# A decode kernel whose last weight matrix arrives in five shrinking pieces, and whose end code is aligned to 256 instructions

## The chip, the cores and the metric

One core of a Trainium2 chip. The metric is device time in microseconds (us) of one execution. Times inside a trace are us from the start of the span, which runs from the first to the last instruction of the program. The measured time is about 2 us longer than the span (1273.29 against 1271.6 us for the profiled run of before).

## The reference, cut to what matters

Two rows of activations pass through grouped-query attention over a key and value cache of 32768 positions, and through a small GELU layer; a gate mixes the two.

```python
q = x @ wq                       # 2 x 1 x 448  ->  16 heads of 256
scores = einsum(q, k) * 256**-0.5    # 8 KV heads, 32768 keys, for each of 2 batch rows
a = einsum(softmax(scores), v).reshape(2, 1, 4096) @ wo     # wo: 4096 x 448
b = gelu(x @ w1 + b1) @ w2 + b2
out = g * a + (1 - g) * b            # g = sigmoid(sum(x * gate_w))
```

The two caches are 537 MB of the 547 MB that must be read.

## The kernel before

SyncE issues every large load on one queue, far ahead of its use: 32 K tiles and 32 V tiles of 8 MB through three slots of SBUF, then the last V tile in three pieces, W2, and WO in four pieces.

```python
    PIECES = (64, 32, 32)                # the last V tile
    WOP = (0, 16, 28, 31, 32)            # WO: bounds of its pieces, in column blocks
    ...
                elif kind == "WO":
                    src = A_wo.rearrange("(p c) n -> p (c n)", p=P)
                    for i in range(len(WOP) - 1):
                        c0, c1 = WOP[i] * Dm, WOP[i + 1] * Dm
                        dma(lambda e, src=src, c0=c0, c1=c1: e.dma_start(wo_v[:, c0:c1], src[:, c0:c1]), f"pW{i}", ("wo", i))
```

TensorE consumes a piece as soon as it is there, two matmuls for each of the 32 blocks:

```python
            def FIN(i):
                E.wait(f"pW{i}", ("wo", i))
                for c in range(WOP[i], WOP[i + 1]):
                    for q in range(2):
                        E.ins(lambda e, c=c, q=q: e.matmul(
                            ps_a[64 * q:64 * q + Bn, :], attnT[:, c:Bn * NC:NC],
                            wo_v[:, c * Dm + q * DQ:c * Dm + (q + 1) * DQ], start=False, ...
```

VectorE, ScalarE and TensorE run a loop over the tiles and then straight code for the end ("tail"). SyncE's program has no loop. VectorE's end, for example:

```python
            for i in range(LAG):
                K(i)
            E.loop((NTILES - LAG) // UNIT, steps, ("dve", ("PT", 0)))
            do_end(NG - 1)               # opens with two copies (selg, o_sb), then waits for the last V pieces
            E.wait("pe", ("OT", NG - 1))
            ...
            E.wait("pe", "FIN")
            E.ins(lambda e: e.tensor_copy(out_sb[:, 0:DQ], ps_a[0:Bn, :]), key="mixd", stream="mix")
```

Of the kernel before, what the change touches and what calls it, by code (L numbers as in the profile page):

```python
# [11 lines left out]
class _Stream:  # L12
    def __init__(self, name, inc):
        self.name = name
        self.inc = inc
        self.count = 0
        self.total = None
        self.events = {}
        self.sem = None
# [7 lines left out]
class _Eng:  # L27
    def __init__(self, sched, name):
        self.s = sched
        self.name = name  # L30
        self.eng = None
        self.log = None
        self.at = None

    def dyn(self, base, step):

        return base if self.at is None else self.at[0] * step + base
# [88 lines left out]
def bass_gated_mix__gqa_block_cached__dense_activation_gelu__decode_kernel(  # L126
# [53 lines left out]
    assert (NTILES - LAG) % UNIT == 0  # L180
    PIECES = (64, 32, 32)
    NC = HD // P
    WOP = (0, 16, 28, 31, 32)
    DQ = Dm // 2
    GELU_C = 0.7978845608028654
    GELU_A = 0.044715
# [7 lines left out]
    for i in range(len(PIECES)):  # L194
        sch.stream(f"pV{i}", 16)
    for i in range(len(WOP) - 1):
        sch.stream(f"pW{i}", 16)
# [3 lines left out]
    with contextlib.ExitStack() as es:  # L201
# [62 lines left out]
        def grp(g):  # L264
            return g // Hkv, g % Hkv
# [74 lines left out]
        def prog_pool(E):  # L340
            E.ins(lambda e: e.memset(ident_b[:], 0.0), key="ms0")
            E.ins(lambda e: e.memset(ident_f[:], 0.0), key="ms1")
            E.ins(lambda e: e.memset(ones_f[:], 1.0), key="ones")
            E.ins(lambda e: e.memset(xm[:], 0.0), key="xm0")
            E.wait("pool", "ms0")
            E.ins(lambda e: e.affine_select(out=ident_b[:], in_=ident_b[:], compare_op=ALU.not_equal, fill=1.0,
                                          base=0, pattern=[[-1, P]], channel_multiplier=1), key="idb")
            E.wait("pool", "ms1")
            E.ins(lambda e: e.affine_select(out=ident_f[:], in_=ident_f[:], compare_op=ALU.not_equal, fill=1.0,
                                          base=0, pattern=[[-1, P]], channel_multiplier=1), key="idf")  # L350
            E.ins(lambda e: e.memset(Abd[:], 0.0), key="A0")
            E.ins(lambda e: e.memset(tsel[:], 0.0), key="t0")
            E.wait("pool", "t0")
            for b in range(Bn):
                E.ins(lambda e, b=b: e.affine_select(
                    out=tsel[:, 136 * b:136 * b + 136], in_=tsel[:, 136 * b:136 * b + 136], compare_op=ALU.not_equal,
                    fill=1.0, base=256 - 128 * b, pattern=[[-1, 136]], channel_multiplier=-8), key=f"ts{b}")

        def prog_sp(E):
            def dma(fn, stream, key):  # L360
                E.ins(fn, key=key, stream=stream)

            for d in order:
                for pd in before_of[d]:
                    E.wait("pe", released(pd))
                kind, idx = d
                if kind == "WQ":
                    parts = [(wq_f, A_wq[0:KC * P, :].rearrange("(p k) n -> p (k n)", p=P), "d_wq0"),
                             (wq_r, A_wq[KC * P:Dm, :].rearrange("p (h n) -> (p h) n", h=2), "d_wq1")]
                    for i, (o, src, _) in enumerate(parts):  # L370
                        dma(lambda e, o=o, src=src: e.dma_start(o, src), "slot0", ("wq", i))
                elif kind == "W1":
                    parts = [(w1_f, B_w1[0:KC * P, :].rearrange("(p k) n -> p (k n)", p=P)),
                             (w1_r, B_w1[KC * P:Dm, :].rearrange("p (h n) -> (p h) n", h=2))]
                    for i, (o, src) in enumerate(parts):
                        dma(lambda e, o=o, src=src: e.dma_start(o, src), "d_w1", ("w1", i))  # L376
                elif kind == "W2":
                    dma(lambda e: e.dma_start(w2_f, B_w2.rearrange("(p f) n -> p (f n)", p=P)), "d_w2", "w2")
# [5 lines that stand above are left out]
                elif d == ("V", LASTV):  # L384
                    src, base, r0 = kv_src(A_v_cache, idx), slot_of[d] * SLOT, 0
                    for i, n in enumerate(PIECES):
                        c0, c1 = r0 * Dh, (r0 + n) * Dh
                        dma(lambda e, c0=c0, c1=c1: e.dma_start(ring[:, base + c0:base + c1], src[:, c0:c1]),
                            f"pV{i}", ("piece", i))
                        r0 += n  # L390
                else:
                    src = kv_src(A_k_cache if kind == "K" else A_v_cache, idx)
                    dma(lambda e, src=src, d=d: e.dma_start(cut(slot_of[d], 0, SLOT), src),
                        f"slot{slot_of[d]}", ("fill", d))
            E.wait_total("mix")
            dma(lambda e: e.dma_start(out[:, 0, :], out_sb), "d_out", "out")
            E.wait_total("d_out")

        def prog_pe(E):
# [147 lines left out]
# [4 lines that stand above are left out]
# [43 lines left out]
            E.wait("dve", "at")  # L594
            for i in range(len(WOP) - 1):
                FIN(i)

        def prog_act(E):
# [35 lines left out]
            def chain(g):  # L634
                E.wait("pe", ("M2", g))
                E.ins(lambda e: e.mul(negm[:, :], ps_m[:, C_BC:C_BC + 1], -SCALE), key=("NM", g))  # L636
                E.wait("act", ("NM", g))
                if g >= 1:
                    E.wait("dve", ("PT", g - 1))
                E.ins(lambda e: e.activation(pexp[:, :].rearrange("p (r i a) -> p i r a", r=CR, i=2),  # L640
                                             ps_s[:, :].rearrange("p (i r a) -> p i r a", i=2, r=CR), ACTF.Exp, bias=negm[:, 0:1], scale=SCALE,
                                             accum_out=lsum[:, 0:1]), key=("X", g))
# [9 lines left out]
            fill_A(1)  # L652
            E.loop(NG - 2, step, ("dve", ("PT", 0)))
            chain(NG - 1)
            E.wait("pe", "FIN")
            E.ins(lambda e: e.copy(out_sb[:, DQ:Dm], ps_a[64:64 + Bn, :]), key="mixa", stream="mix")

        def prog_dve(E):
# [82 lines left out]
            def do_end(g):  # L741
                b, kvh = grp(g)
                if g < NG - 1:
                    E.wait("pe", ("PV", g * NT + NT - 1))
                E.wait("pe", ("OT", g - 1))
                E.wait("dve", "sel")
                E.ins(lambda e: e.tensor_copy(selg[:, :], selw[:, bass.ds(E.dyn(2 * g, 2 * UNIT // NT), 32)]), key=("SG", g))
                E.ins(lambda e: e.tensor_copy(o_sb[:, Dh:Dh + 1], ls3[:, g % 3:g % 3 + 1]), key=("OL", g))
                for n in range(8):
                    w, i = n // 2, n % 2  # L750
                    if g == NG - 1 and i == 0 and w > 0:
                        if w > 1:
                            E.wait("pe", ("PV", LASTV) if w == 3 else ("PVp", w))
                    p = ps_o[:, 512 * w + 256 * i:512 * w + 256 * i + 256]
                    m = mask[:, 4 * i + w:4 * i + w + 1]
                    if n == 0:
                        E.wait("dve", "mask")
                        if g == NG - 1:
                            E.wait("pe", ("PVp", 1))
                        E.ins(lambda e, p=p, m=m: e.tensor_scalar(o_sb[:, 0:Dh], p, m, None, op0=ALU.mult), key=("OS0", g))  # L760
                    else:
                        E.wait("dve", ("OS" + str(n - 1), g))
                        E.ins(lambda e, p=p, m=m: e.scalar_tensor_tensor(  # L763
                            out=o_sb[:, 0:Dh], in0=p, scalar=m, in1=o_sb[:, 0:Dh], op0=ALU.mult, op1=ALU.add),
                            key=(("OS" if n == 7 else "OS" + str(n)), g))
# [15 lines left out]
            for i in range(LAG):  # L781
                K(i)
            E.loop((NTILES - LAG) // UNIT, steps, ("dve", ("PT", 0)))
            do_end(NG - 1)
            E.wait("pe", ("OT", NG - 1))
            E.ins(lambda e: e.reciprocal(rinv[:, :], ps_oa[:, Dh:Dh + 1]), key="ri")
# [55 lines left out]
```

## Time and profile before

| | before |
|---|---|
| time, median of the first 3 runs | 1273.29 us (1273.07 to 1273.34) |
| span of the profiled run | 1271.6 us |
| TensorE / VectorE busy | 55% / 54% |
| main DMA queue | 547.43 MB, 99.6% of 16 engines' span |

The page of the kernel before, its DMA part: for each queue the packets, the megabytes and the time of its packets as a share of 16 DMA engines' span.

```profile
q1 hardware_dynamic: 10804, 547.43, 99.6%
q8 instruction: 8, 0.13, 0.0%
...
q14 instruction: 3, 0.02, 0.0%
```

By this page the packets of queue 1 alone fill 99.6% of the 16 DMA engines' span, so nothing but the start and the end of the stream can be shortened. I read the packets of the two "instruction" queues as fetches of the program itself; with 0.13 and 0.02 MB of 547.59 they are nothing by bytes. Queue 8 I take for TensorE's.

The timeline of the kernel before, its end: start, duration, engine, line, operation, and in brackets the idle time before with what ended it.

```profile
1262.09 2.78 PE L459 MATMUL ps_f<-ring,hT_bf 128*2 128x224 bf16 x28
...
1264.76 2.14 PE L551 MATMUL ps_f<-ring,attnT 128*2 128x224 bf16 x32
...
1267.90 1.70 PE L551 MATMUL ps_f<-ring,attnT 128*2 128x224 bf16 x32 [1.00 <-DMA ring<-in_A_wo_dram]
1269.64 0.34 ACT L656 CAST pexp<-ps_f 2x224 bf16<-2x224 f32 x1 [45.75 <-PE ps_f L551]
1269.64 0.38 DVE L793 CAST pexp<-ps_f 2x224 bf16<-2x224 f32 x1 [7.21 <-PE ps_f L551]
1270.05 0.33 SPq L396 DMA_DIRECT2D out_dram<-pexp  x1
```

TensorE waits 1.00 us for WO's second piece and then has half of WO, 32 matmuls, still to do before the two casts.

### The profile page before, as it was taken

The page shows a single profiled execution, that of the slowest core. Times are in us where ns is not written, and L with a number is a line of the kernel's source. Part 1 is how long each engine was busy: PE and PEld are TensorE (multiplying, and loading weights), DVE is VectorE, ACT ScalarE, POOL GpSimd, SP SyncE. Part 2 cuts the span into 40 slices and gives each one's busy share as a digit, 9 for nine tenths or more (in the row PEclk, how much of TensorE's full clock was granted, in tenths as well). Part 3 has the DMA queues.
Part 4 walks back from the last instruction along what each step waited for, and adds up shares of the span by engine and source line. Part 5 has one row for each costly group of instructions (what it writes and reads, how often), then busy time and mean ns, then how long its engine had stood idle before and what let it go on. Part 6 is the DMA issues. An engine that isn't in the chain of part 4 may idle for free.

```text
span 1271.6 us, 8088 instructions
## 1 busy us (share of the span) xinstructions
PE 698.9 (55%) x4544; PEld 146.0 (11%) x2016; DVE 685.8 (54%) x528; ACT 43.7 (3%) x183; POOL 3.3 (0%) x14
## 2 busy tenths in 40 slices
PE   4566566644466443665544665455664437655465
PEld 3111011100011100111100111000110001111012
DVE  2875537655365563556735466453755636566341
ACT  1000000000000000000000000000000000000000
POOL 1000000000000000000000000000000000000000
PEclk9988788767887777887778887778876778877686
DMA  9999999999999999999999999999999999999998
GB/s 404 441 434 431 429 429 435 431 439 434 431 429 435 437 431 437 435 431 429 433 439 431 437 435 429 431 433 439 431 437 433 431 431 433 439 431 433 437 423 359
DMA packets 10971, 547.59 MB, mean 431 GB/s; under 512 B 1352, under 2 KB 1616, under 8 KB 1872
## 3 DMA queue, kind: packets, MB, share of 16 engines
q1 hardware_dynamic: 10804, 547.43, 99.6%
q8 instruction: 8, 0.13, 0.0%
q10 hardware_dynamic: 156, 0.01, 0.0%
q14 instruction: 3, 0.02, 0.0%
HBM read 547.43 MB, written 0.00 MB: 431 GB/s over the span
## 4 chain that ended last, share of the span: by engine, by line
DMA 63%; DVE 21%; PE 13%; issue 3%; SPq 0%; another core or an unknown queue 0%
DMA ring<-in_A_k_cache_dram 60%; DVE ring L722 19%; PE ps_o L335 4%; PE ps_s L490 3%; PE ps_s L335 3%; DMA ring<-in_A_wo_dram 3%; DVE mx L726 1%; PE ps_o L539 1%; PE ps_m L499 0%; PE ps_m L504 0%; DVE gmax L728 0%; DVE gmx L732 0%; PE ps_f L551 0%; SPq L376 0%
## 5 line engine op out<-in xcount | busy, mean ns | idle before, releaser
L722 DVE STREAM_TRANSPOSE ring<-ring 128x2048 uint32<-128x2048 uint32 x256 | 565.2, 2275 | 390.2 <-DMA ring<-in_A_k_cache_dram 389.9
L490 PE MATMUL ps_s<-ring,Abd 128*128 128x512 bf16 x1024 | 427.0, 417 | 428.7 <-DVE ring L722 428.3
L335 PE MATMUL ps_s<-ring,Abd 128*128 128x512 bf16 x1024 | 423.3, 413 | 0.0
L490 PEld LDWEIGHTS ps_s<-ring,Abd 128*128 128x128 bf16 x1024 | 106.1, 104 | 852.0 <-DVE ring L722 480.1
L335 PE MATMUL ps_o<-ring,PT 128*24 128x512 bf16 x1504 | 112.9, 408 | 0.0
L539 PE MATMUL ps_o<-ring,PT 128*24 128x512 bf16 x544 | 58.1, 427 | 12.6 <-DMA ring<-in_A_v_cache_dram 12.6
L509 PE MATMUL ps_f<-o_sb,selg 128*32 128x257 f32 x32 | 17.0, 634 | 83.5 <-DVE o_sb L763 83.5
L763 DVE SCALAR_TENSOR_TENSOR o_sb<-ps_o,mask,o_sb 128x256 f32<-128x256 f32 x112 | 54.1, 483 | 8.9 <-PE ps_o L539 5.0
L726 DVE TENSOR_REDUCE mx<-ps_s 128x1 f32<-128x1024 f32 x16 | 19.6, 1224 | 59.9 <-PE ps_s L335 59.9
L636 ACT ACTIVATE negm<-ps_m 128x1 f32<-128x1 f32 x16 | 2.7, 171 | 1156.4 <-PE ps_m L504 1156.4
L739 DVE STREAM_TRANSPOSE PT<-pexp 128x1024 bf16<-128x1024 bf16 x16 | 19.9, 1245 | 36.8 <-PE ps_o L335 36.8
L539 PEld LDWEIGHTS ps_o<-ring,PT 128*24 128x24 bf16 x544 | 14.7, 100 | 104.1 <-issue 86.9
L736 DVE COPY ls<-lsum 128x1 f32<-128x1 f32 x16 | 2.5, 154 | 31.8 <-ACT pexp L640 31.8
L630 ACT COPY Abd<-qrep 32x16 bf16 (+1 forms) x128 | 19.4, 199 | 0.6
L640 ACT ACTIVATE pexp<-ps_s,negm 128x1024 bf16<-128x1024 f32 x16 | 17.8, 1113 | 1.7
L499 PE MATMUL ps_m<-ident_f,mx 128*1 128x128 f32 x32 | 6.1, 271 | 21.1 <-DVE mx L726 21.1
L760 DVE TENSOR_SCALAR o_sb<-ps_o,mask 128x256 f32<-128x256 f32 x16 | 7.6, 475 | 17.7 <-PE ps_o L335 17.7
L509 PEld LDWEIGHTS ps_f<-o_sb,selg 128*32 128x32 f32 x32 | 2.9, 139 | 101.6 <-DVE o_sb L763 99.5
L504 PE MATMUL ps_m<-ones_f,gmx 1*128 1x1 f32 x32 | 6.0, 256 | 9.9 <-DVE gmx L732 9.9
L728 DVE TENSOR_REDUCE gmax<-ps_m 1x2 f32<-1x128 f32 x16 | 4.5, 279 | 7.5 <-PE ps_m L499 7.5
L420 PE MATMUL ps_s<-xT,ring 128*128 128x2 bf16 x128 | 3.6, 165 | 8.1 <-DMA ring<-in_A_wq_dram 8.1
L504 PEld LDWEIGHTS ps_m<-ones_f,gmx 1*128 1x128 f32 x32 | 4.7, 183 | 14.6 <-DVE gmx L732 14.6
(76 smaller groups left out, 64.1 us busy)
## 6 DMA issues: line engine op xcount, KB each, us to landing
ring<-in_A_v_cache_dram SPq DMA_DIRECT2D x1, 4096.0 KB, 27.0
ring<-in_A_v_cache_dram SPq DMA_DIRECT2D x2, 2048.0 KB, 33.7
ring<-in_A_wq_dram SPq DMA_DIRECT2D x1, 3072.0 KB, 10.5
ring<-in_A_wo_dram SPq DMA_DIRECT2D x1, 1792.0 KB, 38.2
ring<-in_B_w_dram SPq DMA_DIRECT2D x1, 1568.0 KB, 34.3
ring<-in_B_w_dram SPq DMA_DIRECT2D x1, 1344.0 KB, 13.6
ring<-in_A_wo_dram SPq DMA_DIRECT2D x1, 1344.0 KB, 41.0
ring<-in_A_wq_dram SPq DMA_DIRECT2D x1, 512.0 KB, 11.3
```

Source lines behind the costliest of these rows:

```text
L335: return e.add_instruction(mybir.InstMatmult(name=f"I-{nc.next_id()}", engine=mybir.EngineType.PE, ldweights=False, ins=[e.lower_ap(x), e. ...
L490: fn = lambda e, o=o, x=x, st=st, sp=sp, s=s, w=w: e.matmul(o, a_win(s, w), x, start=st, stop=sp, skip_group_check=True)
L504: E.ins(lambda e: e.matmul(ps_m[:, C_BC:C_BC + 1], gmx[:, :], ones_f[0:1, 0:1], start=True, stop=True), key=("M2", g))
L509: E.ins(lambda e: e.matmul(ps_oa, selg[:, :], o_sb[:, :], start=False, stop=False, skip_group_check=True), key=("OT", g))
L539: fn = lambda e, o=o, x=x, wt=wt, st=st, sp=sp, j=j: e.matmul(o, wt, x, start=st, stop=sp, skip_group_check=True)
L630: E.ins(lambda e, o=o, Q=Q, c=c: e.copy(o[:, :, c:c + 2], qrep[32 * Q:32 * Q + 32, :, bass.ds(E.dyn(2 * g, 2), 2)]), key=(("A", g) if (Q = ...
L640: E.ins(lambda e: e.activation(pexp[:, :].rearrange("p (r i a) -> p i r a", r=CR, i=2), ps_s[:, :].rearrange("p (i r a) -> p i r a", i=2, ...
L722: E.ins(lambda e: e.transpose(k_words(idx, blk), k_words(idx, blk)), key=("T", idx, blk))
L726: E.ins(lambda e: e.tensor_reduce(mx[:, :], ps_s[:, :], AX.X, ALU.max), key=("MX", g))
L739: E.ins(lambda e: e.transpose(PT[:, :], pexp[:, :]), key=("PT", g))
L760: E.ins(lambda e, p=p, m=m: e.tensor_scalar(o_sb[:, 0:Dh], p, m, None, op0=ALU.mult), key=("OS0", g))
L763: E.ins(lambda e, p=p, m=m: e.scalar_tensor_tensor(out=o_sb[:, 0:Dh], in0=p, scalar=m, in1=o_sb[:, 0:Dh], op0=ALU.mult, op1=ALU.add), key= ...
```

## The change

The intent, as read from the code: with pieces that shrink more evenly, fewer blocks are left when a piece lands; and end code that starts at an aligned place is to need no fetch when the end is near. The second is an assumption of the change.

```diff
+    def align(self):
+        if not self.s.plan:
+            self.eng.addr_align(bass.FETCH_BLOCK_INSTRUCTIONS, offset=0, max_nops=0)
...
-    WOP = (0, 16, 28, 31, 32)
+    WOP = (0, 14, 23, 28, 31, 32)
...  # GpSimd: at its end; SyncE: before it waits for the result
+            E.align()
...  # ScalarE: after its loop, before its last cast
             chain(NG - 1)
+            E.align()
             E.wait("pe", "FIN")
...  # VectorE: after its loop, before its tail
             E.loop((NTILES - LAG) // UNIT, steps, ("dve", ("PT", 0)))
+            E.align()
             do_end(NG - 1)
```

The alignment is to 256 instructions, and instead of padding, a branch leads to the next aligned place.

## The prediction

> **What bounds the kernel.** The DMA queue. The page's DMA part: 547.43 MB on queue 1, packets 99.6% of 16 engines' span, 431 GB/s over 1271.6 us; TensorE is 55% busy, VectorE 54%. [...] The change moves no byte less, so only the end after the stream can shrink.
>
> **The tail before** (timeline, waits, semaphore landings in the trace). WO's four pieces (columns 0-16, 16-28, 28-31, 31-32) land whole at 1264.62, 1267.85, 1268.67, 1268.97 us. TensorE does piece 0 from 1264.76 to 1266.9, waits 1.0 us for piece 1 and starts at 1267.90. By then 16 column blocks (32 matmuls) are left, at 0.096 us a block at granted clock 1.0: the last matmul starts at 1269.34 and ends at 1269.60. Then come the casts (0.38), the output DMA's issue (0.33), its landing (1271.19) and the barrier (1271.59): 2.0 us that the change does not touch.
>
> **What the change does to WO.** Pieces end at columns 14, 23, 28, 31, 32. The slowest DMA engine needs 0.27 us a block (3.23 us for 12), so I estimate landings at 1264.1, 1266.5, 1267.9, 1268.7, 1269.0. TensorE: piece 0 from 1264.66 to 1266.5; piece 1 to 1267.4; piece 2 1267.92 to 1268.4; piece 3 1268.74 to 1269.03; piece 4 at 1269.04, the last matmul starting there: 0.3 us sooner than 1269.34, all on the critical path. The fifth issue costs SyncE 0.43 us at 1228, some 36 us ahead of its data: nothing.
>
> **What the alignment does.** One jump each for VectorE (after the loop, about 1231.5), ScalarE (1224), SyncE (1228.5) and GpSimd (4). [...] The instruction queues' packets show what a fetch takes here: 1.0 to 1.1 us for 16 KiB on TensorE's queue, 0.3 to 0.5 us for 8 KiB on the other. At 19.9 us TensorE's matmuls run on through such a fetch[...]. Even a 3 us stall would be free: VectorE next matters at 1250.5 (its 17.7 us wait), ScalarE and SyncE wait over 40 us for the end. I see no fetch stall inside the tail to remove: both casts start 0.04 us after the last matmul. But the last fetches on the other queue are at 1271.44 and 1272.59 us, at the final barrier and after it; the measured time exceeds the span by 1.7 us. [...] I put 0.2 us on it.
>
> **Sum.** 1273.29 - 0.3 - 0.2 = 1272.8 us; range 1271.9 to 1273.5. Within 2%, practically surely.
>
> **What would show it.** The last WO landing stays within 0.1 us of 1268.97; the wait before the last matmuls ends near 1269.0 with two matmuls after it, not 32; span 1271.3. Wrong: landings later by over 0.2 us (one more small DMA costs stream time), or the last matmul still at 1269.3. Alignment: the 8 KiB fetches at 1271.4 and 1272.6 move earlier; if the time falls by more than the span, they held up the end.
>
> **What would make it wrong.** A low granted clock in the last 4 us (0.187 us a block, as at 1264-1265.7); [...]drift of the stream rate, where 0.1% is 1.3 us.

What is cut from this text, and from the expectations below, is marked. The sum came to 1273.29 - 0.3 (the pieces) - 0.2 (the alignment) = 1272.8 us. The 0.2 us: no trace showed that the two late fetches hold up the program's end. "TensorE's queue" is queue 8, "the other" queue 14.

## More of the kernel before

VectorE's wait at the entry of its tail, from the list of waits (engine, tile, line, what ended it; us in total, times, longest):

```profile
DVE selg L747 <- PE ps_f L509: 1.2, 1, 1.2
```

## The result

| | before | changed |
|---|---|---|
| time, median of 4 runs | 1273.32 us (1273.07 to 1273.70) | 1274.43 us (1274.31 to 1274.56) |
| span of the profiled run | 1271.6 us | 1272.8 us |
| last piece of WO landed | 1268.97 us | 1270.35 us |

The ratio is 1.0009 (95% interval 0.9991 to 1.0026). Here and below a ratio is worked out from the fast runs of the two kernels in the same rounds, so it is not quite the ratio of the medians. The interval holds 1. Still, the four times lie clear above all four of before, and outside the predicted range of 1271.9 to 1273.5. The span separates the two better than the time: it is 1272.5 to 1272.8 us in all nine runs of the changed kernel (these four and five later ones), and 1271.0 to 1271.6 in all 27 runs of before that later rounds timed. The profiled run of before, with 1271.6, is thus one of its longest.

The DMA part of the page of the changed kernel:

```profile
q1 hardware_dynamic: 10948, 547.43, 99.6%
q8 instruction: 8, 0.13, 0.0%
q14 instruction: 10, 0.08, 0.0%
```

Queue 14 has 10 instruction fetches instead of 3. The same part for the stretch from 1226 to 1250 us, of the kernel before and then of the changed kernel:

```profile
q1 hardware_dynamic: 366, 10.03, 97.2%
```

```profile
q1 hardware_dynamic: 352, 9.85, 96.1%
q14 instruction: 6, 0.05, 0.5%
```

Six of them fall into this stretch; the kernel before has none there. (Two more, at 7.3 and 12.3 us, follow GpSimd's jump, and one that before has at 1271.4 us is gone.) The six take 0.5% of the DMA time of the stretch.

The timeline of the changed kernel, its end:

```profile
1263.46 2.77 PE L466 MATMUL ps_f<-ring,hT_bf 128*2 128x224 bf16 x28
...
1266.02 4.75 PE L558 MATMUL ps_f<-ring,attnT 128*2 128x224 bf16 x64
1270.82 0.34 ACT L664 CAST pexp<-ps_f 2x224 bf16<-2x224 f32 x1 [47.53 <-PE ps_f L558]
1270.82 0.38 DVE L802 CAST pexp<-ps_f 2x224 bf16<-2x224 f32 x1 [7.03 <-PE ps_f L558]
1271.23 0.34 SPq L403 DMA_DIRECT2D out_dram<-pexp  x1
```

Everything from the last V piece on is 1.2 to 1.4 us later. In this run TensorE also happened to run at half clock (granted clock 0.5) from 1255.5 to 1269.1 us, so it reached WO's blocks without a wait; its last matmul still ended only 0.43 us after WO's last landing.

VectorE's wait at the entry of its tail, changed kernel:

```profile
DVE selg L755 <- issue: 7.2, 1, 7.2
```

The jump makes VectorE stand for 7.2 us ("issue": it waits for nothing that the profile shows). It branches at 1230.53 us and its next instruction is at 1237.98.

What the views do not print is in the trace's semaphore records. Each of these loads has 16 reports there, and TensorE waits for the last: in the kernel before, the 15th report of WO's second piece came at 1267.21 us, the 16th at 1267.85, and the first matmul on it started at 1267.90. These are the last three reports of the same loads:

```
                 before                          changed
V piece 0        1246.00  1246.16  1246.78       1245.99  1246.19  1248.14
V piece 2        1255.79  1255.92  1256.57       1255.77  1255.99  1257.92
last WO piece    1268.17  1268.33  1268.97       1268.19  1268.41  1270.35
```

The third-last and second-last reports are within 0.1 us of where they were. The last is 1.35 to 1.38 us later than the last was before, and 1.9 us behind the second-last. I read the 16 reports as one from each of the 16 DMA engines; the latest of them decides.

**Which engine is it?** The trace gives no engine for a packet. But the packets from 70 to 1262 us, all 9383 of the changed kernel and all 9372 of before, can be chained into just 16 streams in which each packet starts 3 to 5 ns before the last one's end (around a fetch it can be up to 15 ns) and exactly 8 data packets lie between two reports. I take each stream for one DMA engine. Three streams of the changed kernel, each number the start of one report, F the start of an 8 KiB fetch:

```
A: 72.98  F 87.50  93.31 ... 286.81  F 306.16  306.47  326.48 ... 1216.65  F 1235.99  1236.31  F 1241.83  1247.66
B: 72.69           92.04 ...                                      1214.35  F 1226.45  F 1231.97  1235.08  1244.79
C: 73.07           92.43 ... 285.95            305.30  324.65 ... 1214.95                        1234.30  1244.00
```

Stream C has no fetch, and its reports are 19.35 us apart. Stream A loses 0.98 us to the fetch at 87.50 us (20.33 instead of 19.35), about 1 us to that at 306.16, and 1.93 us to the two at 1235.99 and 1241.83. B loses 1.38 us to two. In 890 us only 0.13 us of it was made up: A was 1.83 us behind C at 326.48 us and still 1.70 us behind at 1216.65. So A enters the tail late, by the two fetches of 900 and 1100 us before. This is the stream that decides the end.

Below, an engine has "time in hand" when it reports earlier than the latest of the 16. In the kernel before, VectorE's stream reported at 1216.60 us and had 0.66 us in hand: the latest, at 1217.26, was a stream that had carried a fetch of TensorE at 88.42 us. That is why A loses 1.93 us to its last two fetches and the end only 1.4.

The records show where a fetch's cost goes beyond its own packet of some 0.32 us, though not why: the data packet right behind it is longer too. On A the 64 KiB packet at 87.82 us took 3.08 us instead of 2.42, and the 32 KiB packets behind the last two fetches 1.87 us each instead of 1.22. On B the packets behind took 2.80 us instead of 2.42, so B loses less.

A's last two fetches follow VectorE's branch; B's follow ScalarE's branch at 1222.10 us. Two more, at 1244.01 and 1249.01 us on a third stream, follow SyncE's branch at 1239.95 us. SyncE's branch is that late because its fifth WO issue stood for 11.8 us. Why is not shown; in all four runs with five pieces that issue ended 1.8 to 2.1 us after the last full V tile had landed, and in e1 below such a stand of 10.6 us cost nothing that shows (span 0.26 us shorter than before).

### The profile page after: what moved, and what is told of

The parts are those of the page before. It is cut to its first block, busy times and chain, and to the rows that moved or that the text cites. A ratio compares the mean times of both kernels' runs of the same rounds, so it can differ in the third digit from the quotient of the medians.

```text
span 1272.8 us, 8093 instructions
## 1 busy us (share of the span) xinstructions
PE 705.8 (55%) x4544; PEld 147.6 (12%) x2016; DVE 685.9 (54%) x528; ACT 43.7 (3%) x183; POOL 3.3 (0%) x14
## 3 DMA queue, kind: packets, MB, share of 16 engines
q1 hardware_dynamic: 10948, 547.43, 99.6%
## 4 chain that ended last, share of the span: by engine, by line
DMA 62%; DVE 18%; PE 16%; issue 3%; SPq 0%; another core or an unknown queue 0%
DMA ring<-in_A_k_cache_dram 59%; DVE ring L730 16%; PE ps_s L497 5%; PE ps_s L340 5%; PE ps_o L340 4%; DMA ring<-in_A_v_cache_dram 3%; PE ps_o L546 1%; DVE mx L734 1%; PE ps_m L511 0%; PE ps_m L506 0%; PE ps_f L558 0%; DVE gmax L736 0%; DVE gmx L740 0%; PE ps_f L466 0%
## 5 line engine op out<-in xcount | busy, mean ns | idle before, releaser
L340 PE MATMUL ps_o<-ring,PT 128*24 128x512 bf16 x1504 | 115.9, 417 | 0.0
L546 PE MATMUL ps_o<-ring,PT 128*24 128x512 bf16 x544 | 58.4, 428 | 16.0 <-DMA ring<-in_A_v_cache_dram 16.0
```

Of the source, the lines that this page charges most:

```text
L340: return e.add_instruction(mybir.InstMatmult(name=f"I-{nc.next_id()}", engine=mybir.EngineType.PE, ldweights=False, ins=[e.lower_ap(x), e. ...
L546: fn = lambda e, o=o, x=x, wt=wt, st=st, sp=sp, j=j: e.matmul(o, wt, x, start=st, stop=sp, skip_group_check=True)
```

## The experiments

Theory A: a jump's fetches take time on one of 16 independent DMA engines, and the latest engine ends the stream. Rivals: R1, the fifth WO piece costs stream time; R2, TensorE's half clock; R3, VectorE's standing still; R4, a fixed cost for every fetch; R5, only VectorE's jumps cost; R6, only late fetches cost. Every kernel gave correct results and was timed in 5 rounds beside the kernel before. The edits are shown against the changed kernel, and only the part that is new; those with 4 pieces also have the bounds of before. The alignment is that of no engine in e6, of VectorE alone in e7, e8 and e10, and of ScalarE alone in e9.

Results of all runs:

| kernel | WO pieces | 8 KiB fetches 1220 to 1260 us | last WO landing, and its last report behind the one before | span, mean | span of before, same rounds | median time (before) |
|---|---|---|---|---|---|---|
| e1_wo5 | 5 | 1 | 1268.55, 0.31 | 1270.90 | 1271.16 | 1272.95 (1273.43) |
| e2_align4 | 4 | 6 | 1270.16, 1.63 | 1272.88 | 1271.16 | 1274.92 (1273.43) |
| e3_dve | 4 | 2, VectorE's | 1270.47, 1.89 | 1272.96 | 1271.16 | 1274.88 (1273.43) |
| e4_nodve | 4 | 4, others' | 1268.67, 0.13 | 1271.22 | 1271.16 | 1273.31 (1273.43) |
| e5_wo5_nodve | 5 | 4, others' | 1268.76, 0.17 | 1270.86 | 1271.17 | 1272.67 (1273.06) |
| e6_busy | 4 | 0 | 1268.49, 0.18 | 1271.22 | 1271.17 | 1273.43 (1273.06) |
| e7_dve128 | 4 | 1, VectorE's | 1269.14, 0.64 | 1271.86 | 1271.17 | 1273.81 (1273.06) |
| e8_dve2 | 4 | 4, VectorE's | 1272.18, 3.65 | 1274.84 | 1271.17 | 1276.71 (1273.06) |
| e9_act3 | 4 | 6, ScalarE's | 1270.37, 1.87 | 1273.00 | 1271.23 | 1274.78 (1273.37) |
| e10_early | 4 | 0, one more early | 1269.37, 0.89 | 1272.06 | 1271.23 | 1273.99 (1273.37) |
| e11_after | 5 | 6 | 1270.30, 1.18 | 1272.58 | 1271.23 | 1274.39 (1273.37) |

The landing is that of one profiled run; the span is the mean of 5 runs, and of 9 for before.

**e1_wo5: the pieces alone.**

```diff
-        if not self.s.plan:
+        if not self.s.plan and self.name in ():
             self.eng.addr_align(...)
```

> WO in 5 pieces alone, no alignment. Theory A (the jumps' instruction fetches delay one DMA engine): no 8 KiB fetch between 1220 and 1270 us, the last WO piece lands within 0.2 us of 1269.0, the last of the 16 completions of each late piece at most 0.7 us behind the one before it, and the time is 0.1 to 0.5 us below the kernel before. Rival R1 (the fifth piece itself costs stream time): last landing near 1270, time about 1 us above the kernel before. Rival R2 (TensorE happened to run at half clock through the tail): time goes with the granted clock after 1262 us, landings unchanged.

Measured: ratio 0.9996, the span 0.26 us shorter (1270.90 against 1271.16), as A said, and R1 falls. One fetch did occur, at 1242.83 us, which I had not expected; whose it is, is not shown. It cost nothing that shows. The last landing, 1268.55 us, was earlier than the 1268.8 to 1269.2 I had expected: in this run no engine was by itself as late as in the profiled run of before. The timeline of e1_wo5, its end:

```profile
1267.47 0.65 PE L558 MATMUL ps_f<-ring,attnT 128*2 128x224 bf16 x10 [0.32 <-DMA ring<-in_A_wo_dram]
...
1268.34 0.55 PE L558 MATMUL ps_f<-ring,attnT 128*2 128x224 bf16 x8 [0.22 <-DMA ring<-in_A_wo_dram]
1268.93 0.34 ACT L664 CAST pexp<-ps_f 2x224 bf16<-2x224 f32 x1 [45.47 <-PE ps_f L558]
```

After its last wait TensorE has 8 matmuls left instead of 32, and the casts start 0.38 us after the last landing (1268.93 - 1268.55) instead of 0.67 (1269.64 - 1268.97). That is the gain.

**e2_align4, e3_dve, e4_nodve: the alignment alone, of all four engines, of VectorE, of the other three.**

```diff
-    WOP = (0, 14, 23, 28, 31, 32)
+    WOP = (0, 16, 28, 31, 32)
...
+        if not self.s.plan and self.name in ('dve',):            # e3; ('pool', 'sp', 'act') in e4
```

> Alignment of the four engines alone, WO in the 4 pieces of before. A: six 8 KiB fetches between 1226 and 1250 us as in the changed kernel, one of 16 completions of each late piece 1.9 us behind the others, last WO landing about 1270.3 us, time 1.0 to 1.6 us above the kernel before. R1: time as before or lower.

> Alignment of VectorE alone, 4 pieces. A: two 8 KiB fetches near 1236 and 1242 us, both on one DMA engine, which loses 1.4 to 1.9 us. If that is again an engine that was late before, the last landing is near 1270 and the time about 1 us above the kernel before; if it is an early one, the landing stays at 1269 and the time does not rise. R1 and R2 expect no rise from this.

> Alignment of SyncE, ScalarE and GpSimd without VectorE, 4 pieces. A: four 8 KiB fetches in the tail, two each on two DMA engines. In the changed kernel these two were engines that were early (their completions came 1.5 to 2.3 us before the last), so I expect the landing to stay within 0.3 us of 1269 and the time within 0.4 us of the kernel before; the time beyond the span is to tell whether an aligned end of the program is shorter (1.8 us in the changed kernel, 2.7 in the profiled run of before).

Measured: the four engines' alignment lengthens the span by 1.72 us, VectorE's alone by 1.80, the others' by 0.06 (ratios 1.0013, 1.0011, 1.0000). The DMA part of e3_dve and of e4_nodve, 1226 to 1250 us, shows that e4 even has more fetches:

```profile
q14 instruction: 2, 0.02, 0.2%
```

```profile
...
q14 instruction: 4, 0.03, 0.3%
```

So the number of fetches does not decide (R4 falls), and neither does the total of DMA time. In the chained streams of both runs the fetches sit as in the changed kernel: VectorE's two on a stream that reported at 1216.80 us, among the last; e4's four, two each, on streams that reported at 1214.47 and 1214.84, the earliest and the third earliest. Those had over 2 us in hand.

**e5_wo5_nodve: the changed kernel without VectorE's jump.**

```diff
+        if not self.s.plan and self.name in ('pool', 'sp', 'act'):
```

> The changed kernel without VectorE's jump (5 pieces; SyncE, ScalarE, GpSimd aligned). If VectorE's jump alone makes the changed kernel slow: last WO landing within 0.3 us of 1268.8, no completion over 0.7 us behind the one before, span near 1271, time 1272.7 to 1273.3, that is 0.2 to 0.6 us below the kernel before. If the other jumps matter too in this combination (SyncE's fifth issue moves its jump later), the landing is over 1269.3.

Measured: ratio 0.9996, the span 0.31 us shorter than before, five times from 1272.52 to 1272.89 us against nine from 1272.89 to 1273.50. One word taken away turns the loss into the gain of the pieces.

**e6_busy: VectorE late by work, without a jump.**

```diff
-            E.align()
+            for i in range(20):
+                E.ins(lambda e: e.memset(busy[:, :], 0.0), key=f"bz{i}")
+                E.wait("dve", f"bz{i}")
             do_end(NG - 1)
```

> No jump. 20 memsets of a scratch tile keep VectorE busy for about 6 us at the place of the jump, so its selector copy comes as late as in the changed kernel (7 us idle there). Rival R3 (what costs is VectorE's late start of the tail): time about 1.4 us above the kernel before. Theory A: no further fetch, the landing stays at 1269 and the time within 0.3 us of the kernel before.

Measured: the memsets took 9.0 us, more than meant, and the selector copy came at 1241.73 us, 3.7 us later than in the changed kernel. The span is 0.05 us from that of before, the ratio 1.0000. R3 falls: 9.0 us of delay on VectorE cost nothing here. From the waits of e6_busy, VectorE's first use of the last V tile:

```profile
DVE o_sb L769 <- PE ps_o L341: 7.9, 1, 7.9
```

Even so late it waits 7.9 us more for TensorE. The median time is 0.37 us up, a little over the 0.3 that I had allowed; span and ratio show no rise. By the way this run too had the half clock, from 1253.4 to 1267.0 us, and R2 gets nothing from it: the span is that of before, and the landing no later. Conversely, e9 and e11 below had full clock from 1267.0 us on and lose 1.77 and 1.35 us of span. In the changed kernel's profiled run half clock cost at most 0.17 us: its casts start at 1270.82 us, those of e11_after, with full clock from 1267.0 and the same landing within 0.05, at 1270.65.

**e7_dve128 and e8_dve2: the dose.** In e7 the alignment is to 128 instructions, in e8 a second jump follows the two copies.

```diff
-            self.eng.addr_align(bass.FETCH_BLOCK_INSTRUCTIONS, offset=0, max_nops=0)
+            self.eng.addr_align(128, offset=0, max_nops=0)          # e7
...
                 E.ins(lambda e: e.tensor_copy(o_sb[:, Dh:Dh + 1], ...), key=("OL", g))
+                if g == NG - 1:                                      # e8
+                    E.align()
```

> VectorE alone, 4 pieces, but aligned to 128 instructions instead of 256. [...] A: then only one fetch follows the jump, near 1232 to 1237 us, VectorE idles under 3 us instead of 7.2, and the DMA engine that carries the fetch loses 0.3 to 1.0 us instead of 1.9: last landing 1269.0 to 1269.6 and time 0 to 0.8 us above the kernel before, below VectorE aligned to 256.

> VectorE alone, 4 pieces, with a second jump of the same kind right after the two copies that open its tail: four 8 KiB fetches. A: if the second pair falls on the same DMA engine as the first, that engine loses some 3.8 us, the last landing is near 1272 and the time some 3 us above the kernel before; if on another, that one loses 1.4 to 1.9 us, and the landing moves past the 1270.4 of one jump only if that engine was late by itself. If time follows the number of jumps by a fixed cost each whatever the engine (rival R4), it is 2 x 1.45 us above the kernel before.

Measured: with 0, 1, 2 and 4 fetches of VectorE in the tail (e6, e7, e3, e8) the span is 0.05, 0.69, 1.80 and 3.67 us above that of before; the ratios of e7 and e8 are 1.0005 and 1.0029. In e8 the late engine is 3.65 us behind the next. In e7 VectorE hardly stops. Its wait at the entry of the tail:

```profile
DVE selg L755 <- PE ps_f L516: 1.2, 1, 1.2
```

This is the 1.2 us of before: VectorE's branch took 0.56 us to its next instruction, and the one fetch did not hold it up. Whether the code it jumps to was there already is not shown. So a jump stalled VectorE for 7.1 us (e3) or not at all (e7); its fetches cost time either way (1.80 and 0.69 us of span). R4's sum for e8 (2.9 us) was too low.

**e9_act3: an engine that starts with time in hand.**

```diff
             chain(NG - 1)
+            for i in range(3):
+                E.align()
+                E.ins(lambda e, i=i: e.copy(spare[:, i:i + 1], selw[:, i:i + 1]))
```

> ScalarE alone, 4 pieces, three jumps in a row at the end of its loop: six 8 KiB fetches between about 1226 and 1255 us, all on ScalarE's one DMA engine. In the runs so far that engine completed its share some 2.3 us before the last one, and two fetches (1.4 us) cost nothing. If the end is set by the latest of 16 independent DMA engines, six fetches at 0.7 to 0.95 us make 4.2 to 5.7 us, so this engine ends 1.9 to 3.4 us after the others: landing 1270.9 to 1272.4, time 1.7 to 3.4 us above the kernel before. Rival R4 (0.92 us for every fetch, whatever the engine): 5.5 us above. Rival R5 (only VectorE's jumps cost): no rise.

Measured: all six fetches, and no other, on one stream; against a neighbour that reported at the same time before them (1214.54 and 1214.55 us) it is 4.14 us late after them, 0.69 each. It had some 2.3 us in hand, and ends 1.87 us behind the other fifteen. The span is 1.77 us longer, ratio 1.0012; the median is 1.41 us up and the landing is 1270.37, both below the ranges I gave. R5 (nothing) and R4 (5.5 us) fall. Two fetches on this engine cost nothing (e4), six cost 1.8 us: that is a maximum over engines, not a sum.

**e10_early: the jump 1150 us before the end.**

```diff
             for i in range(LAG):
                 K(i)
+            E.align()
             E.loop((NTILES - LAG) // UNIT, steps, ("dve", ("PT", 0)))
-            E.align()
             do_end(NG - 1)
```

> VectorE alone, 4 pieces, but the jump stands ahead of its loop (about 55 to 75 us) and not ahead of its tail: the loop then starts a block, and I expect three 8 KiB fetches in the first 310 us[...] against two before, and none near the end. If a DMA engine never makes up for a fetch (the queue always has work for it), VectorE's engine is about 1 us later at the end than in the kernel before: landing 1269.2 to 1269.8, time 0.4 to 1.0 us above. Rival R6 (the stream makes up for a fetch within some slots, only those of the last 40 us cost): landing 1268.6 to 1269.0 and time within 0.3 us of the kernel before.

Measured: VectorE stands 4.65 us before its loop. The DMA part of e10_early and then of before, 70 to 320 us:

```profile
...
q14 instruction: 3, 0.02, 0.0%
```

```profile
...
q14 instruction: 2, 0.02, 0.0%
```

One fetch more between 70 and 320 us, none in the tail. The stream of VectorE's fetches is the latest of 16 by 0.86 us at 1218 us and by 0.89 us at the end; the span is 0.83 us longer, ratio 1.0006. R6 falls: a fetch more at 85 to 91 us costs at 1269 us no less (0.83) than one at 1236 us (e7, 0.69).

**e11_after: the changed kernel again.**

> The changed kernel again, for a comparison on this chip: last WO landing near 1270.3 us, VectorE's DMA engine 1.9 us behind, time 1.0 to 1.4 us above the kernel before.

Measured: ratio 1.0010, span 1.35 us longer, last landing 1270.30 us. VectorE's engine was only 1.18 us behind the next, because another engine was late in this run: the one with TensorE's fetch at 88.52 us, which reported at 1217.40 us. The landing is what counts, and it is the expected one.

## Why the prediction was wrong

- *"The change moves no byte less, so only the end after the stream can shrink"*: right, but the stream could grow, and I did not ask whether it would.
- *The pieces, "0.3 us sooner ... all on the critical path"*: right. e1 shows 0.26 us of span, and the casts 0.29 us nearer to the landing. Only the detail was off: after its last wait TensorE had eight matmuls left, not two.
- *"The fifth issue costs SyncE 0.43 us"*: wrong by itself (it stood 11.8 us), and of no account, since SyncE waits some 30 us more for the result.
- *"Even a 3 us stall would be free"*: right, and beside the point. VectorE stood 7.2 us, and in e6 a delay of 9.0 us left the span within 0.05 us of that of before.
- **The step that failed is the alignment's cost, which I put at nothing but a gain of 0.2 us.** I had the duration of a fetch ("0.3 to 0.5 us for 8 KiB"), and spent it only on the engine that waits for the code. It is also time of one DMA engine (0.69 to 0.98 us for a fetch in the streams here), in a kernel that I had just called DMA-bound. The missing term is +1.72 us of span (e2 against before): two fetches of VectorE at 0.9 us each, on an engine with little or nothing in hand (0.66 us in the profiled run of before; 0.35, 0.19 and 0 in those of e4, e5 and e6). Spread over all engines the six fetches are nothing (6 packets of 0.32 us in 16 engines' 45 us, 0.3%); but each of these loads has 16 reports, and TensorE waits for the last one.
- *"The last WO landing stays within 0.1 us of 1268.97"*: wrong, 1270.35. The check that I named for this, "landings later by over 0.2 us", fired, but for another cause than the one I tied to it (one more small DMA).
- *The end of the program*: the late 8 KiB fetches at 1271.4 and 1272.6 us did go. Whether this shortens the time beyond the span stays open: the mean of time less span was 2.37, 2.00 and 2.14 us for before in its three sets of rounds, and 1.83 (e5), 2.19 (e4) and 2.11 (e11) with the fetches gone. The spread of before is as large as any gain.

The sum as measured, in span: -0.26 (pieces, e1) + 1.72 (alignment, e2) = +1.46, against +1.35 for both (e11).

That the stall-free e7 and the early e10 cost too, that e4 costs nothing and e9 costs only beyond what its engine had in hand, is shown. Not shown is why the data packet behind a fetch is longer, so that a fetch whose own packet takes some 0.32 us costs its engine 0.7 to 1.0 us, nor which of the 16 engines will be late by themselves: besides VectorE's, those with an early TensorE fetch were, and a few from the start of the stream on.

The better kernel is e5_wo5_nodve or e1_wo5, about 0.3 us of span better than before; their times cannot be told apart from each other.

## What to carry to other kernels

In a kernel that keeps all DMA engines busy, as this one does (99.6%), look for the load's last report, not for the queue's mean. Here an 8 KiB transfer on one engine delayed that engine's later reports by more than its own time (0.7 to 1.0 us against a packet of 0.32 us), at 85 to 91 us (e10) as well as at 1236 us (e7), and the end with them, unless that engine had time in hand (e4). Before you align or branch code after a stream has started, count the fetches it causes. A stall can be free for the engine that stands (7.2 us in the changed kernel, 9.0 us of work in its place in e6) while the fetches behind it are not: VectorE's two cost 1.80 us of span (e3).

## What else these traces show of instruction fetches

- An 8 KiB fetch cost the DMA engine that carried it 0.69 us (e9) to 0.98 us (changed kernel, at 87.50 us), a 16 KiB fetch of TensorE 1.55 us (before, at 133.28 us: 20.90 us between two reports instead of 19.35). It was still missing some 900 to 1130 us later: in the kernel before, from the first report after 72 us to the last before 1218 us, the ten streams without a fetch took 1141.64 to 1141.86 us, the five with one 16 KiB fetch 1143.22 to 1143.36, and VectorE's, with two of 8 KiB, 1143.62.
- In these traces the fetches on queue 8 are 16384 bytes, those on queue 14 8192, and an alignment of VectorE to 128 instructions caused one fetch and no stop where one to 256 caused two and 7.1 us (e7, e3).
- Under this full DMA load VectorE's branch took 7.4 us to its next instruction in the changed kernel (1230.53 to 1237.98), of which 5.5 us passed before the fetch's packet started (1235.99); in e7 the same took 0.56 us.
- In the chained traces VectorE's four fetches (changed kernel) are all on one engine and ScalarE's six in e9 on one; the five 16 KiB fetches of before from 88 to 288 us are on five different ones.
